# Another order of steps in attention, and the last unit's addition split over two engines, in an adaLN block with segment-memory attention and a SwiGLU network

## Chip, cores and metric

One core of a Trainium2 chip. The metric is the device time of one execution in microseconds (us); before the change its median is 1815.66 us over 3 runs (1815.52 to 1815.91).

## What is computed

All data are float32. 2048 tokens of width 576 pass a modulated layer norm, attention with 32 heads of 18 elements in four segments of 512 tokens, a projection with a gated residual, a second modulated layer norm and a SwiGLU network of width 4608. The reference, cut to what matters:

```python
mod = (_silu(c) @ w_mod).reshape(c.shape[0], 6, 1, -1)
sa, ca, ga, sb, cb, gb = ...
h = _layernorm(x) * (1 + ca) + sa
x = x + ga * _A_ref(h, wq, wk, wv, wo, beta)
h = _layernorm(x) * (1 + cb) + sb
x = x + gb * _B_ref(h, w_gate, w_up, w_down)      # (silu(h @ w_gate) * (h @ w_up)) @ w_down
...
for s in range(N):                                # _A_ref: four segments
    a_dot = softmax(qs @ ks^T * scale + mask) @ vs
    a_mem = (phi(qs) @ M) / (phi(qs) @ z + 1e-6)  # memory of the segments before
    o = g * a_mem + (1.0 - g) * a_dot
    M = M + phi(ks)^T @ vs
    z = z + sum(phi(ks))
...
return o @ wo
```

The gated output is the line `o = g * a_mem + (1.0 - g) * a_dot`.

## The kernel before, in words

Matrix products keep float32 accuracy by splitting each operand into a high and a low part (names ending in h and l) and adding three products. The program has three stages: projections of segments 0 to 2, attention (with the projections of segment 3, the output projection of finished segments and the preparation of the network's inputs woven in), and, behind the output projection of the last segment, the network.

**Attention** runs over 32 units, each one segment and four heads. Its order of work is written out by hand in the table ORDER: one string for each unit, with a token for each step. `<` and `>` ahead of a token move it to the unit before or behind. The tokens that matter here:

- `r` is a step of the maxima: one PSUM bank of scores (L689), whose row maxima VectorE takes with a custom reduction (L211). It works for the unit two further on. `s` is a step of the softmax: a bank of scores (L718) that ScalarE turns into exponentials (L725, L727); after some of them GpSimd cuts off the masked triangle (L730). When an `s` and an `r` stand next to each other, their matrix products are issued alternately.
- `m` transposes a unit's maxima (L235), `n` copies them (L239) and sends them by a DMA on SyncE's queue into two rows of that unit's `qs` tile (L194), which its `s` steps read.
- `V0123` multiplies the exponentials with the values (`av`, L744), `E` evacuates the product (`avs`, L757), `c` transposes it (`px`, L766) and `d` is comb_b: a reciprocal (L774), a product with it into `tmp` (L781) and the addition of `tmp` into the gated output `o` (L782). For segment 0 there is no addition. For the units behind, GpSimd adds; for the last unit, number 31, VectorE does.
- `M0` to `M3` and `X` are a half tile of the output projection (`pw`, L846) and its addition to the residual (`xr`, L851), `R S T Z z` make its operands (transposes L819 and L802, high parts L825, low parts L829), `l p x` are the second layer norm, and `y0` to `y131` are the steps that prepare the first half of the network's inputs: loads (L1143, L1146), transposes (L1155), scaling (L1150), GpSimd's sums (L1209), casts (L1134), low parts (L1117, L1119) and stores (L1123, L1125).

All banks of attention are one ring of eight in PSUM: a new one waits until the one eight places back has been read.

**Behind attention** the last segment's output projection stands in fixed order: TensorE transposes the gated output of the first 128 tokens (`pto`, four transposes L819), its last 64 columns for all tokens (`ptr`, L802) and the next 128 tokens, and then runs the projection's products (`pw`, L846). ScalarE casts the first transposes (`hh`, L825) before the products can begin. GpSimd's queue holds three sums for the network (L1221) and then four sums of weights (L1343). SyncE's queue loads weights (L1321) and the network's inputs `y` (L1308, L1309); the second of the weight tiles lies in memory that attention frees last. The first product of the network is an L1388 at 550.02 us.

Of the kernel before, what the change touches and what calls it, by code (L numbers as in the profile page):

```python
# [7 lines left out]
F32 = mybir.dt.float32  # L8
# [3 lines left out]
ALU = mybir.AluOpType  # L12
# [3 lines left out]
P = 128  # L16
S = 2048
D = 576
# [86 lines left out]
def block(ctx: ExitStack, tc: tile.TileContext, x, wqk, wv, wo, beta, wgu, wd, c, w_mod, wm01, out):  # L105
    nc = tc.nc
# [69 lines left out]
    NU = len(units)  # L176
    mcol, pmt, mrow, qe = {}, {}, {}, {}
    B1 = [[(3, h)] for h in (1, 0, 3, 2)] + [[(2, h), (0, h)] for h in (1, 0, 3, 2)] + [[(1, 1), (1, 3)], [(1, 0), (1, 2)]]
# [152 lines left out]
    with ExitStack() as p1:  # L331
# [3 lines left out]
        wk = pool(p1, "wk1", 2)  # L335
# [432 lines left out]
    def comb_b(u):  # L768
        if u < 0:
            return  # L770
        s, q = units[u]
# [1104 lines left out]
```

## Time and profile before

| | us |
|---|---|
| median of 3 runs | 1815.66 |
| the profiled execution's own time | 1815.06 |
| its span, first to last instruction | 1813.3 |
| attention's last `av` products end | 525.04 |
| first product of the last segment's projection | 532.52 |
| first product of the network | 550.02 |
| TensorE at half of its clock | 529.16 to 535.98 |
| mean granted clock over the span | 0.998 |

All times within the execution are counted from the span's start. PE is TensorE, PEld its loading of weights, DVE VectorE, ACT ScalarE, POOL GpSimd, SP SyncE. In a view of instructions in order of time, a line holds start, duration, engine, source line, operation, tiles (written<-read), sizes and count; a bracket at its end gives how long the engine stood idle ahead of it, and who ended that. A view of stretches gives the busy time of each engine in each stretch, with the number of its instructions in brackets, then the granted TensorE clock and the DMA engines' share.

### The profile page before, as it was taken

The numbers are of one execution on the slowest core, as the hardware profiler recorded it, in microseconds if no ns is written. First come the engines' busy times: TensorE is split into PE (matmuls) and PEld (weight loads), VectorE is DVE, ScalarE is ACT, GpSimd is POOL, SyncE is SP. The second block draws the span as 40 slices with busy tenths as digits, with TensorE's granted clock in tenths as the row PEclk, the third lists the DMA queues.
The fourth block names the chain that finished last, engine by engine and source line by source line (L and its number), as shares of the span: only waits on it lengthen the run. The fifth ranks groups of instructions, "written<-read, shape, count | busy, mean of one in ns | idle before, by whom it ended". The sixth has DMA issues, their size and how long they took to land.

```text
span 1813.3 us, 31111 instructions
## 1 busy us (share of the span) xinstructions
PE 1789.0 (99%) x11061; PEld 1515.2 (84%) x11061; DVE 1480.0 (82%) x3277; ACT 949.5 (52%) x2073; POOL 490.9 (27%) x707
## 2 busy tenths in 40 slices
PE   8999999999989999999999999999999999999999
PEld 5888867767778888888888888888888888888888
DVE  7567589999968888889888898668888888888886
ACT  6444578778866445444544444434544544544542
POOL 3000146555660544544454444100000000000000
PEclk9999999999999999999999999999999999999999
DMA  8678766577678455555544543594324324323331
GB/s 287 234 239 281 236 195 180 165 195 214 179 238 269 160 185 175 164 172 188 190 144 140 174 155 121 193 293 138 107 79 130 107 80 130 107 81 129 107 103 53
DMA packets 178563, 304.51 MB, mean 168 GB/s; under 512 B 25304, under 2 KB 108184, under 8 KB 176616
## 3 DMA queue, kind: packets, MB, share of 16 engines
q1 hardware_dynamic: 151032, 248.66, 43.9%
q10 hardware_dynamic: 27376, 53.86, 8.5%
q8 instruction: 88, 1.44, 0.3%
q14 instruction: 67, 0.55, 0.1%
HBM read 188.42 MB, written 113.33 MB: 166 GB/s over the span
## 4 chain that ended last, share of the span: by engine, by line
PE 68%; DVE 2%; DMA 1%; POOL 1%; issue 1%; ACT 1%; ACTq 0%; DVEq 0%
PE A L1388 24%; PE pd L1516 13%; PE C L1388 12%; PE pd L1497 10%; PE B L1388 6%; PE pw L846 1%; DMA y<-yD 1%; DVE wr L1338 0%; DVE wl L1353 0%; DVE dl L1378 0%; PE pt L1288 0%; ACT Pt L725 0%; PE av L744 0%; POOL Pt L730 0%; DVE acc L1526 0%
## 5 line engine op out<-in xcount | busy, mean ns | idle before, releaser
L1388 PE MATMUL A<-y,wh 128*128 128x512 f32 x1152 | 406.1, 393 | 1.2 <-ACT B L1434 0.9
L1388 PEld LDWEIGHTS A<-y,wh 128*128 128x128 f32 x1152 | 216.6, 188 | 46.2 <-ACT B L1434 2.4
L1353 DVE TENSOR_TENSOR wl<-O,wh 128x256 fp32r<-128x256 f32 x504 | 248.0, 497 | 2.1 <-ACT wh L1352 1.6
L211 DVE CUSTOM_DVE_ANT_0 junk<-s,tri 128x384 bf16<-128x384 f32 (+3 forms) x512 | 218.6, 486 | 25.2 <-PE s L689 12.7
L1388 PE MATMUL A<-y,wl 128*128 128x512 f32 x576 | 226.9, 394 | 0.0
L1502 DVE TENSOR_TENSOR acc<-acc,pd 128x576 f32<-128x576 f32 x216 | 162.4, 752 | 59.0 <-PE pd L1497 51.5
L1388 PE MATMUL C<-y,wh 128*128 128x512 f32 x576 | 203.0, 393 | 0.5 <-DVE cu L1411 0.5
L1352 ACT CAST wh<-O 128x256 fp32r<-128x256 f32 x504 | 197.6, 405 | 1.5 <-DMA yD<-st 1.2
L1526 DVE TENSOR_TENSOR acc<-acc,pd 128x576 f32<-128x576 f32 x156 | 116.9, 750 | 89.7 <-PE pd L1516 89.3
L1516 PE MATMUL pd<-dh,ah 128*128 128x288 f32 x640 | 189.0, 295 | 0.5 <-DVE x L1520 0.5
L1516 PE MATMUL pd<-dh,al 128*128 128x288 f32 x640 | 189.1, 296 | 0.0
L1516 PE MATMUL pd<-dl,ah 128*128 128x288 f32 x640 | 188.8, 295 | 0.0
L1343 POOL TENSOR_TENSOR O<-O 128x384 f32<-128x384 f32 x132 | 149.1, 1144 | 139.0 <-DMA O<-in_wgu_dram 64.3
L1457 ACT CAST ah<-sg 128x512 fp32r<-128x512 f32 x192 | 119.2, 621 | 77.9 <-DVE sg L1412 71.4
L725 ACT ACTIVATE Pt<-s 128x512 f32<-128x512 f32 x256 | 136.0, 599 | 21.4 <-PE s L718 15.2
L1458 DVE TENSOR_TENSOR al<-sg,ah 128x512 fp32r<-128x512 f32 x192 | 136.4, 710 | 10.4 <-ACT ah L1457 10.2
L1497 PE MATMUL pd<-dh,ah 128*128 128x288 f32 x448 | 133.0, 297 | 0.0
L1497 PE MATMUL pd<-dh,al 128*128 128x288 f32 x448 | 132.5, 296 | 0.0
L1497 PE MATMUL pd<-dl,ah 128*128 128x288 f32 x448 | 132.3, 295 | 0.0
L1516 PEld LDWEIGHTS pd<-dl,ah 128*128 128x128 f32 x640 | 120.5, 188 | 7.2
L1516 PEld LDWEIGHTS pd<-dh,ah 128*128 128x128 f32 x640 | 120.8, 189 | 6.8 <-DVE x L1520 0.8
L1388 PEld LDWEIGHTS C<-y,wh 128*128 128x128 f32 x576 | 108.3, 188 | 21.5 <-DVE cu L1411 1.2
(412 smaller groups left out, 4336.6 us busy)
## 6 DMA issues: line engine op xcount, KB each, us to landing
O<-in_wgu_dram SPq DMA_DIRECT2D x36, 768.0 KB
O<-oD SPq DMA_DIRECT2D x36, 512.0 KB
oD<-O ACTq DMA_DIRECT2D x34, 512.0 KB
ks<-kD SPq DMA_DIRECT2D x64, 216.0 KB
qs<-qD SPq DMA_DIRECT2D x64, 216.0 KB
O<-in_wgu_dram SPq DMA_DIRECT2D x36, 384.0 KB
rD<-wr ACTq DMA_DIRECT2D x36, 336.0 KB
wr<-rD SPq DMA_DIRECT2D x35, 336.0 KB
```

Source lines behind the costliest of these rows:

```text
L211: nc.vector.tensor_tensor_reduce(junk[:, :n], bank[:, o:o + n], tri[:, L - n:], 1.0, -3e38, op0=ALU.add, op1=ALU.max, accum_out=mcol[u][0] ...
L725: nc.scalar.activation(pt[:, h], bank, AF.Exp, scale=SCALE)
L1343: eng.tensor_tensor(o[:, d], o[:, a], o[:, b], op=op)
L1352: nc.scalar.copy(wh, o)
L1353: later.append(lambda: nc.vector.tensor_tensor(wl, o, f32(wh), op=ALU.subtract))
L1388: nc.tensor.matmul(bank, lhsT=a, rhs=b, start=(first and n == 0), stop=(n == 6), skip_group_check=not first)
L1457: nc.scalar.copy(ah, src)
L1458: later.append(lambda: nc.vector.tensor_tensor(al, src, f32(ah), op=ALU.subtract))
L1497: nc.tensor.matmul(pd[:, i, :288], lhsT=a[:, tk], rhs=w, start=(k == 0), stop=(k == 2))
L1502: nc.vector.tensor_tensor(o, o, pd[:, :, :288], op=ALU.add)
L1516: nc.tensor.matmul(pd[:, i, :288], lhsT=a[:, tk], rhs=w, start=(k == 0), stop=(k == 5))
L1526: nc.vector.tensor_tensor(o, o, pd[:, :, :288], op=ALU.add)
```

## The change

The first part rewrites ORDER from the second string on. It has the same tokens for the same units in all (the `y` steps have no unit), in another sequence; 260 pairs of neighbouring `s` and `r` become 259. TensorE's instructions stay 9,012 rows of the same matrix products. One string, the old and the new, and the second part in full:

```diff
-    "s s r s s y52 r r m U n V0123 l y59 E s r y83 s r s r M0 M1 y71 r s s r r s M2 y94 M3 X y106 y95 >r",
...
+    "s y52 s s r p y83 y49 y66 r s <E y84 V0123 y59 E r s s r s r M0 y106 M1 r s r s r s y77 M2 >U M3 y94 y95 y72 X y78 y119 >r",
...
         else:
-            tmp = wk.tile([P, 320], F32, tag="tmp", name="tmp")[:, :288].rearrange("p (i h z) -> p i h z", i=4, h=4)
+            last = u == NU - 1
+            tmp = (wk.tile([P, D], F32, tag="woraw", name="tmp", bufs=1) if last else
+                   wk.tile([P, 320], F32, tag="tmp", name="tmp"))[:, :288].rearrange("p (i h z) -> p i h z", i=4, h=4)
             nc.vector.tensor_tensor(tmp, v[:, :, :, :DH], rb, op=ALU.mult)
-            (nc.vector if u == NU - 1 else nc.gpsimd).tensor_tensor(dst, dst, tmp, op=ALU.add)
+            k = 3 if last else 4 if u == NU - 3 else 0
+            if k:
+                nc.vector.tensor_tensor(dst[:, :k], dst[:, :k], tmp[:, :k], op=ALU.add)
+            if k < 4:
+                nc.gpsimd.tensor_tensor(dst[:, k:], dst[:, k:], tmp[:, k:], op=ALU.add)
```

Each unit's output has four token blocks of 72 columns. VectorE now adds the first three blocks of unit 31 and GpSimd the fourth; unit 29 (NU - 3) is added by VectorE alone, where GpSimd did it before; the other units stay with GpSimd. The last unit's `tmp` takes a buffer of its own (the tag `woraw`, one buffer that the layer norm's output uses earlier), instead of the two that the units take in turn. The new lines shift the numbers: L782 becomes L786 (VectorE) and L788 (GpSimd), L781 becomes L783, and every line behind is 6 higher (L846 becomes L852).

VectorE's instructions at the end of attention, before, up to the low part of the projection's first operand (`r` and `tmp` belong to units 29, 30 and 31, in this order; `yo` and `yq` are low parts for the network):

```order
L774 RECIPROCAL r_8393<-px 128x16
L781 TENSOR_TENSOR tmp<-px,r_8393 128x288
L1119 TENSOR_TENSOR yo<-yh_5574,yo 32x256
L774 RECIPROCAL r_8404<-px 128x16
L781 TENSOR_TENSOR tmp<-px,r_8404 128x288
L774 RECIPROCAL r_8416<-px 128x16
L781 TENSOR_TENSOR tmp<-px,r_8416 128x288
L782 TENSOR_TENSOR o_6413<-o_6413,tmp 128x4x72
L829 TENSOR_TENSOR hl<-pto,hh 128x512
```

VectorE at the same place in the changed kernel:

```order
L774 RECIPROCAL r_8371<-px 128x16
L783 TENSOR_TENSOR tmp<-px,r_8371 128x288
L786 TENSOR_TENSOR o_6401<-o_6401,tmp 128x4x72
L1123 TENSOR_TENSOR yo<-yh_5626,yo 128x256
L1125 TENSOR_TENSOR yo<-yh_5627,yo 32x256
L774 RECIPROCAL r_8404<-px 128x16
L783 TENSOR_TENSOR tmp<-px,r_8404 128x288
L774 RECIPROCAL r_8416<-px 128x16
L783 TENSOR_TENSOR tmp<-px,r_8416 128x288
L786 TENSOR_TENSOR o_6401<-o_6401,tmp 128x3x72
L835 TENSOR_TENSOR hl<-pto,hh 128x512
```

Unit 29's addition and one more low part have come in ahead of unit 30; the last addition has three blocks instead of four.

GpSimd at the end of attention, before (the x2 are units 29 and 30; L1221 are the three sums for the network):

```order
L730 AFFINE_SELECT Pt<-Pt 128x4x128 x4
L1209 TENSOR_TENSOR yh_5571<-yh_5571,yh_5573 128x256
L1209 TENSOR_TENSOR yh_5571<-yh_5571 96x256
L1209 TENSOR_TENSOR yh_5571<-yh_5571,yh_5574 96x256
L782 TENSOR_TENSOR o_6413<-o_6413,tmp 128x4x72 x2
L1221 TENSOR_TENSOR ys<-yh_5571,yh_5572 128x512
L1221 TENSOR_TENSOR o_6413<-yh_5571,yh_5573 128x512
L1221 TENSOR_TENSOR ys<-yh_5571,yh_5574 96x512
```

GpSimd at the same place in the changed kernel:

```order
L730 AFFINE_SELECT Pt<-Pt 128x4x128 x4
L1215 TENSOR_TENSOR yh_5624<-yh_5624,yh_5626 128x256
L1215 TENSOR_TENSOR yh_5624<-yh_5624,yh_5627 96x256 x2
L788 TENSOR_TENSOR o_6401<-o_6401,tmp 128x4x72
L788 TENSOR_TENSOR o_6401<-o_6401,tmp 128x72
L1227 TENSOR_TENSOR ys<-yh_5624,yh_5625 128x512
L1227 TENSOR_TENSOR o_6401<-yh_5624,yh_5626 128x512
L1227 TENSOR_TENSOR ys<-yh_5624,yh_5627 96x512
```

Unit 29's addition is gone, and a quarter of unit 31's stands ahead of the three sums, which therefore wait for the last `tmp`.

TensorE where unit 31's maxima are transposed (`pmt`), before; the next `s` reads the tile of the unit ahead, `qs_996`, and three of unit 31's own (`qs_2347`) follow behind 16 `av` and 12 more `s`:

```order
L766 MATMUL px<-ident,avs 128x128 x4
L235 MATMUL pmt<-ident,mc 32x128
L718 MATMUL s_8163<-qs_996,ks_997 128x512
L718 MATMUL s_8166<-qs_996,ks_997 128x512
L718 MATMUL s_8173<-qs_996,ks_997 128x512
L718 MATMUL s_8176<-qs_996,ks_997 128x512
L744 MATMUL av<-Pt,vq_5821 32x512 x4
```

TensorE at the same place in the changed kernel:

```order
L766 MATMUL px<-ident,avs 128x128 x4
L1161 MATMUL pt<-ident,yq 96x128 x4
L235 MATMUL pmt<-ident,mc 32x128
L744 MATMUL av<-Pt,vq_5633 32x512 x4
L744 MATMUL av<-Pt,vq_5633 32x384 x4
L744 MATMUL av<-Pt,vq_5633 32x256 x4
L744 MATMUL av<-Pt,vq_5633 32x128 x4
L718 MATMUL s_8191<-qs_996,ks_997 128x512
```

The `av` products moved ahead of the four `s`; behind those, a half tile of the projection (14 `pw`) and four transposes now stand ahead of unit 31's first `s` as well, which before stood behind it.

56 rows, old and new, of the table ORDER are left out of this document.

## Prediction

> **What bounds the kernel now.** First the page's busy times: TensorE works 99% of the span.
>
> ```profile
> PE 1789.0 (99%) x11061; PEld 1515.2 (84%) x11061; DVE 1480.0 (82%) x3277; ACT 949.5 (52%) x2073; POOL 490.9 (27%) x707
> ```
>
> So a gain must come from TensorE's idle time or from its clock; the change leaves its products as they are. Next, the stretches: attention (to 525), the last segment's projection (525 to 550), the network's start.
>
> ```profile
> 215.00:525.00 310.00, 305.67 (x2867) 219.81 (x2865) 268.49 (x1127) 237.13 (x487) 176.10 (x379) 1.00 0.65 188
> 525.00:550.00 25.00, 21.11 (x144) 20.24 (x141) 18.47 (x32) 11.49 (x23) 10.50 (x11) 0.86 1.01 351
> 550.00:570.00 20.00, 20.00 (x89) 16.38 (x88) 17.23 (x36) 13.94 (x33) 0.00 (x0) 1.00 0.79 245
> ```
>
> Attention loses 4.3 of 310 us. The 25 us behind it lose 3.9 us and run at 0.86 of the clock. That joint is where the change's second part lies. TensorE there, in order of time:
>
> ```profile
> 520.47 4.57 PE L744 MATMUL av<-Pt,vq 128*32 128x512 f32 x64
> 525.85 0.66 PE L766 MATMUL px<-ident,avs 128*128 128x128 f32 x4 [0.22 <-ACT avs L757]
> 530.72 0.45 PE L819 MATMUL pto<-ident,o 128*128 128x128 f32 x1 [3.27 <-DVE o L782]
> 532.52 0.59 PE L846 MATMUL pw<-woh,hh 128*128 128x288 f32 x1
> ```
>
> And VectorE, GpSimd and ScalarE at that place:
>
> ```profile
> 525.66 0.26 DVE L774 RECIPROCAL r<-px 128x16 f32<-128x16 f32 x1 [3.24 <-PE px L766]
> 526.03 0.46 DVE L781 TENSOR_TENSOR tmp<-px,r 128x288 f32<-128x288 f32 x1
> 526.54 0.26 DVE L774 RECIPROCAL r<-px 128x16 f32<-128x16 f32 x1
> 527.10 0.46 DVE L781 TENSOR_TENSOR tmp<-px,r 128x288 f32<-128x288 f32 x1 [0.30 <-POOL o L782]
> 527.59 2.98 DVE L782 TENSOR_TENSOR o<-o,tmp 128x288 f32<-128x288 f32 x1
> ```
>
> ```profile
> 526.28 1.54 POOL L782 TENSOR_TENSOR o<-o,tmp 128x288 f32<-128x288 f32 x2
> 527.78 1.26 POOL L1221 TENSOR_TENSOR ys<-yh,yh 128x512 f32<-128x512 f32 x1
> 529.00 1.26 POOL L1221 TENSOR_TENSOR o<-yh,yh 128x512 f32<-128x512 f32 x1
> 530.22 1.47 POOL L1221 TENSOR_TENSOR ys<-yh,yh 96x512 f32<-96x512 f32 x1
> ```
>
> ```profile
> 531.20 0.58 ACT L825 CAST hh<-pto 128x512 fp32r<-128x512 f32 x1 [5.41 <-PE pto L819]
> ```
>
> The chain is: transposes of unit 31, reciprocal, `tmp`, addition, transposes `pto`, cast, products. VectorE's addition takes 2.98 us beside GpSimd's sums and ends 0.35 us after the third of them began. Its own work is a fraction of that: the low parts 128x256 from two SBUF tiles take 0.40 us, and when one of them meets a GpSimd sum it takes 0.83 us, which is the rest of that one sum plus its own time.
>
> ```profile
> L1117 DVE TENSOR_TENSOR mbd<-yh,mbd 128x256 fp32r<-128x256 f32 x4 | 1.6, 403 | 0.0
> ```
>
> ```profile
> 513.25 0.83 DVE L1117 TENSOR_TENSOR yo<-yh,yo 128x256 fp32r<-128x256 f32 x1 [2.22 <-ACT yo L1134]
> 513.05 1.62 POOL L1209 TENSOR_TENSOR yo<-yh,yo 128x256 f32<-128x256 f32 x2
> ```
>
> Last, the clock: half of it was granted for 6.82 us, shown here in halves, with stretches of the same length around them:
>
> ```profile
> 522.33:525.74 3.41, 3.30 (x52) 1.46 (x43) 0.17 (x2) 2.11 (x4) 3.33 (x6) 1.00 0.90 275
> 525.74:529.16 3.42, 1.20 (x7) 0.78 (x7) 2.93 (x5) 0.05 (x1) 3.42 (x5) 1.00 0.95 319
> 529.16:532.57 3.41, 1.85 (x10) 1.74 (x10) 2.10 (x2) 1.10 (x2) 3.41 (x3) 0.50 1.01 405
> 532.57:535.98 3.41, 3.41 (x16) 3.41 (x15) 1.38 (x2) 1.69 (x4) 3.01 (x4) 0.50 1.02 339
> 535.98:539.40 3.42, 3.42 (x29) 3.42 (x28) 2.37 (x5) 0.88 (x2) 0.00 (x0) 1.00 1.04 359
> ```
>
> A stretch with 1.20 us of work was followed by half the clock, one with 1.85 us did not end that, a full one did. At half clock 16 products run where 29 run at the full one.
>
> **The change part by part.** *The last addition.* (1) Unit 31's `tmp` no longer waits for GpSimd: it starts behind its reciprocal, at 526.83 instead of 527.10, 0.27 us earlier. (2) Three blocks of four on VectorE: between 0.34 us (216/256 of 0.403) and 2.98 us (the row as it is, if GpSimd keeps it out again). I take 0.36 us, near the lower end: GpSimd's sums can no longer start ahead of it, since its quarter, which waits for the same `tmp`, stands before them. That saves 2.62 us. `pto` then resumes at 530.72 - 0.27 - 2.62 = 527.83. (3) GpSimd's quarter: between 0.20 us (a quarter of the 0.80 us in the row below) and 0.80 us. Only the last `ptr` transpose needs it. I take 0.25 us behind VectorE's part, so 527.95 us; TensorE gets there at about 528.2 us, so it costs nothing, and 0.5 us at the upper end.
>
> ```profile
> L782 POOL TENSOR_TENSOR o<-o,tmp x23: 788/803/912, 321.8 to 527.0; 128x288 f32<-128x288 f32 x23
> ```
>
> The Trainium skill, page "SBUF — State Buffer", section "Who interferes with whom", says that a VectorE instruction with two SBUF inputs and a GpSimd instruction that reads SBUF exclude each other, and that the later one waits for the whole of the earlier. By that rule sharing runs no two parts at once, so 0.36 + 0.25 us would be no better than VectorE's undivided 0.46 us. The trace agrees that the two exclude each other, but the 2.98 us spans two whole sums, one more than the rule's words give.
>
> (4) From the resumed `pto` to the first product: 1.80 us now, at half clock. At full clock four transposes take 0.36 us of TensorE (the next product starts at 505.34), so the nine left take 0.81 us; the cast is later: 0.33 us for the transpose at full clock, 0.03, then 0.58 and 0.05 us, about 1.0 us. Saved 0.8 us.
>
> ```profile
> 504.98 0.60 PE L819 MATMUL pto<-ident,o 128*128 128x128 f32 x4
> 505.34 0.38 PE L846 MATMUL pw<-woh,hh 128*128 128x288 f32 x1
> ```
>
> (5) Products from 532.57 to 535.98 at full clock: 3.41 x (1 - 16/29) = 1.53 us saved, if the clock stays. In the stretch that now has 1.20 us of work, the nine transposes and some products would add 1.3 us: 2.5 of 3.41. Between 1.85, which did not raise the clock, and the 3.30 that kept it, the trace does not say; I take it as kept, because work that keeps the clock need not be as much as work that raises it.
>
> *Unit 29's addition* goes from GpSimd (0.80 us) to VectorE (0.46 us alone, up to about 1.3 us behind one GpSimd instruction). VectorE's 3.24 us of idle time ahead of 525.66 hides it; without that cover unit 30's reciprocal would be up to 1.3 us late, and all of (1) behind it. GpSimd then comes to unit 30's addition without a backlog.
>
> *What starts earlier.* GpSimd's three sums start about 0.2 us later (527.95 against 527.78) and VectorE reads them long after. The second weight load on SyncE's queue is issued right as the addition ends (530.57) and comes earlier with it:
>
> ```profile
> 530.65 0.33 SPq L1321 DMA_DIRECT2D O<-in_wgu_dram  x1
> 550.02 0.39 PE L1388 MATMUL A<-y,wh 128*128 128x512 f32 x1
> ```
>
> The DMA engines are full from 525 to 550 (share 1.01, 351 GB/s). What is loaded there is three `xr` and a fourth (288 KB each), two weight tiles (768) and four `y` (1216): 7.55 MB, about 22 us from 523.2, done at about 546. The last `y` is first read some 4.8 us into the network, 549.7 us if all moves up by 5.2 us. So 3 to 4 us of slack remain; TensorE's only wait of that kind now is 0.2 us, late in the program.
>
> *The new order.* TensorE's work is equal, so only its waits can change. Its twelve listed waits in attention before the joint add to 4.1 us; first, third and last:
>
> ```profile
> PE s L718 <- ACT Pt L727: 0.7, 1, 0.7
> ...
> PE s L718 <- DMA qs<-mr: 0.4, 2, 0.2
> ...
> PE s L689 <- DVE mx L211: 0.2, 1, 0.2
> ```
>
> If all vanish, 4.1 us are gained; as much again might come at other places, since VectorE is at 268.49 of 310 us and a bank read late stops the ring. The wait for unit 31's maxima goes (0.2 us: 16 `av` and more stand in its place), and I find no term that outweighs it; I take 0, with both ends for the range.
>
> **Sum:** 0.27 + 2.62 + 0.8 + 1.53 = 5.2 us. The profiled execution of 1815.06 us (a span of 1813.3 with 1.8 around it) would take 1809.8 us; the shown median is 0.6 us above it, so 1815.66 - 5.2 = **1810.5 us**.
>
> **The rivals.** *A, the clock falls all the same.* From the last `av` (525.04) to the first product (528.85) lie 3.8 us with transposes alone, longer than one stretch. For it: the stretch with seven transposes and no product was followed by half the clock. Against it: the work in it would double. Price: one stretch at half clock, 1.53 us, so 1812.0 us. The Trainium skill, page "TensorE: Matmul & The Clock Gate", section "Part 4: PE-mode transpose", says that transposes do not count as busy as products do, which would make A the case; no stretch here tells the kind of work apart from its amount.
>
> *B, the sharing does not do what it says.* GpSimd's unit 30 addition starts behind `tmp` at about 526.56 and ends at 527.36, just as VectorE's addition starts (527.32). If GpSimd's quarter and sums then follow without a gap, VectorE is kept out as before: 2.62, 0.8 and 1.53 us stay lost, and 1815.4 us results. Against it: at 513.25 VectorE got in between two GpSimd sums.
>
> *C, the order brings new waits* of 2 to 4 us. For it: TensorE's waits are few now, so that a new sequence can hardly remove many, and between two units' `av` more of VectorE's work may gather. Price 3 us: 1813.5 us.
>
> *D, slower.* One mechanism: the ring of eight banks, where VectorE's reductions and low parts hold banks that `s` and `r` need. VectorE has 310 - 268.49 = 41.5 us free in 31 units, 1.3 us each. If the sequence lets it fall behind in every unit, each costs TensorE a wait; from 0.3 us a unit (9 us in all, against 5.2 us gained) it is over 0.2% slower: about 1819.5 us. Against it: the single waits now are 0.2 to 0.7 us, twelve in 31 units.
>
> **How the numbers follow.** Forecast 0.50 (1808.4 to 1812.0), A 0.20, B 0.08, C 0.15, D 0.07. The range goes from 1808.0 (2.5 us of attention's waits gone as well) to 1815.4 (B), and leaves out D and the tails. A difference of 0.2%, 3.6 us, is about what a measurement of this kernel can tell from no change, so faster ends at 1812.0 us: the forecast and half of A, 0.60; half of A, B and C, 0.33; D, 0.07.
>
> **What would show it.** In the changed profile: the addition of 128x216 on VectorE near 0.36 us and no wait over 0.5 us of `pto` for it (1, 2); the first product about 3.8 us behind the last `av` instead of 7.5 (4); no half clock near 529 us (5; if it is there, A); GpSimd's sums behind the quarter (if VectorE's addition is over 2 us, B); attention's `av` end at 525.0 within 1 us (if it is later, C or D); no DMA wait of the network's first products. The prediction is wrong if attention itself moves by more than 2 us either way.

## Result, and the profile after

| | before | after |
|---|---|---|
| median, us | 1815.47 (1813.66 to 1818.79, 20 runs) | 1810.8 (1807.86 to 1815.57, 20 runs) |
| profiled execution, us | 1815.06 | 1811.66 |
| its span, us | 1813.3 | 1809.9 |

The ratio is 0.9975, with a 95% interval from 0.9968 to 0.9982: the changed kernel is faster by about 4.7 us, over the 0.2% (3.6 us) that the prediction calls the least a measurement can tell; the interval's weak end, 0.18%, lies just under it. (The ratios, here and below, are not exactly the quotients of the two medians.) Its median came out 0.3 us from the forecast. The parts did not, and most of what follows is about them.

The page's busy times of the changed kernel:

```profile
PE 1784.7 (99%) x11061; PEld 1512.8 (84%) x11061; DVE 1479.9 (82%) x3278; ACT 947.8 (52%) x2073; POOL 492.3 (27%) x707
```

The three stretches that were shown of before:

```profile
215.00:525.00 310.00, 306.67 (x2892) 221.85 (x2890) 274.83 (x1141) 238.61 (x492) 179.06 (x381) 1.00 0.66 191
525.00:550.00 25.00, 22.52 (x154) 21.27 (x155) 20.56 (x39) 13.72 (x29) 9.30 (x9) 1.00 1.01 362
550.00:570.00 20.00, 18.86 (x82) 15.15 (x81) 16.92 (x34) 12.14 (x29) 0.00 (x0) 1.00 0.89 303
```

The clock of the 25 us behind attention is 1.00 instead of 0.86. But TensorE is still idle for 2.5 us there, and for 1.1 us in the 20 us behind, which had no idle time before. Fixed stretches hide what moved, since the work in them shifts, so the table below cuts each trace at the same instructions: the first product of segment 3's projections, the end of the last `av`, the first product of the last segment's projection, and the network's 1st, 141st, 1501st and 2001st product, counting the products of L1388 (L1394 in the changed kernel) alone. But for the last `av`, whose end counts, the marks are starts.

| stretch, us | before | after | difference |
|---|---|---|---|
| stage 1 (its code is unchanged) | 194.31 | 196.66 | +2.35 |
| attention, to the last `av` | 330.73 | 326.30 | -4.43 |
| joint, to the projection's first product | 7.48 | 3.85 | -3.63 |
| projection, to the network's first product | 17.49 | 18.12 | +0.63 |
| network, products 1 to 140 | 38.75 | 39.67 | +0.92 |
| to product 1500 | 496.40 | 496.04 | -0.36 |
| to product 2000 | 182.19 | 183.35 | +1.16 |
| the rest | 545.98 | 545.95 | -0.03 |

They add up to the 3.4 us between the spans. Stage 1 takes 192.8 to 198.8 us in the fourteen profiles of this study although no kernel changes it, and 192.8 to 196.7 us in the three of the changed kernel (after, e4, e11). Part of that is the clock: in the changed kernel, e7 and e10 half of it was granted for 3.4 or 6.8 us from 151 us on, and these three have the longest stage 1 (196.7 to 198.8 us; the other eleven 192.8 to 194.8). This is why each step is judged by its own stretch and not by the span.

**The joint.** TensorE of the changed kernel in order of time:

```profile
522.89 0.66 PE L766 MATMUL px<-ident,avs 128*128 128x128 f32 x4
523.83 0.66 PE L766 MATMUL px<-ident,avs 128*128 128x128 f32 x4 [0.28 <-ACT avs L757]
525.42 0.72 PE L825 MATMUL pto<-ident,o 128*128 128x128 f32 x4 [0.93 <-DVE tmp L783]
525.97 0.60 PE L808 MATMUL ptr<-ident,o 128*64 128x128 f32 x4
...
526.81 0.40 PE L852 MATMUL pw<-woh,hh 128*128 128x288 f32 x1
```

VectorE and GpSimd there:

```profile
524.81 0.46 DVE L783 TENSOR_TENSOR tmp<-px,r 128x288 f32<-128x288 f32 x1
525.30 0.38 DVE L786 TENSOR_TENSOR o<-o,tmp 128x216 f32<-128x216 f32 x1
```

```profile
524.43 1.45 POOL L788 TENSOR_TENSOR o<-o,tmp 128x288 f32<-128x288 f32 x2
525.84 1.27 POOL L1227 TENSOR_TENSOR ys<-yh,yh 128x512 f32<-128x512 f32 x1
...
531.86 4.88 POOL L1349 TENSOR_TENSOR O<-O 128x384 f32<-128x384 f32 x4 [2.22 <-DMA O<-in_wgu_dram]
```

VectorE's three blocks take 0.38 us; GpSimd's sums start at 525.84, behind both additions. The last row is new: the sums of weights (L1349) wait 2.22 us for the first weight tile. GpSimd does not come to them earlier than before: counted from the last `av`, it ends the third sum at 6.65 us in the kernel before and at 6.68 us here. Before, the weights were there in time; here they are not.

**The clock at the joint.** In each of the fourteen traces the changes of the clock lie whole multiples of 3.413 us apart (in the changed kernel 11.38, 151.32, 154.74 and 1810.20 us). Cut by that grid, there are six stretches at full clock that hold transposes and no product: one in the changed kernel and in e8, which the full clock followed, and one in e2, e3, e5 (below, in this order) and the kernel before (525.74:529.16 in the prediction, 1.20 us of work), which half of it followed. The experiments are described further down.

```profile
523.38:526.79 3.41, 2.20 (x18) 1.69 (x16) 1.81 (x5) 1.01 (x3) 3.27 (x5) 1.00 0.89 274
```

```profile
522.19:525.60 3.41, 2.11 (x18) 1.66 (x17) 1.81 (x5) 1.01 (x3) 3.27 (x5) 1.00 0.84 258
```

```profile
521.70:525.11 3.41, 1.61 (x11) 0.93 (x9) 2.30 (x6) 0.67 (x1) 3.41 (x5) 1.00 0.84 258
```

```profile
520.96:524.37 3.41, 1.52 (x11) 1.10 (x12) 2.56 (x4) 0.11 (x1) 3.41 (x4) 1.00 0.88 270
```

```profile
526.95:530.37 3.42, 0.41 (x4) 0.44 (x5) 2.87 (x1) 0.07 (x1) 3.42 (x4) 1.00 0.95 329
```

So here transposes alone kept the clock, with 2.11 us of work in a stretch or more, and lost it with 1.61 us or less.

**The give-back.** ScalarE's cast of these sums, and TensorE in the projection behind it:

```profile
536.77 0.62 ACT L1343 CAST wr<-O 96x512 fp32r<-96x512 f32 x1 [3.69 <-POOL O L1349]
```

```profile
541.15 0.37 PE L852 MATMUL pw<-woh,hh 128*128 128x288 f32 x1 [2.06 <-DVE xr L857]
```

In the program's order, the projection's next cast (`hh`, L831) stands behind that cast on ScalarE, and runs at 537.60. VectorE waits 1.97 us for it:

```profile
538.21 0.69 DVE L835 TENSOR_TENSOR hl<-pto,hh 128x512 fp32r<-128x512 f32 x1 [1.97 <-ACT hh L831]
```

Behind this low part follow VectorE's addition to the residual (`xr`, 540.55), which empties TensorE's bank, and TensorE, after 2.06 us of waiting. The weight tile is late because of SyncE's queue:

```profile
522.35 0.36 SPq L1129 DMA_DIRECT2D yD<-yo  x1
523.22 0.31 SPq L1131 DMA_DIRECT2D yD<-yo  x1
523.58 1.39 SPq L819 DMA_DIRECT2D xr<-in_x_dram  x3
525.09 0.36 SPq L1327 DMA_DIRECT2D O<-in_wgu_dram  x1
```

The load goes behind two stores of network inputs (`yo`), 2.13 us after the last `av` (522.96). In the kernel before it went 0.56 us after it: the new order does these last steps later, relative to attention's end. In the network's first 140 products TensorE then waits 1.14 us for VectorE (`cu`, L1417), where it waited 0.48 us before.

### The profile page after: what moved, and what is told of

The parts are those of the page before. It is cut to its first block, busy times and chain, and to the rows that moved or that the text cites. A ratio compares the mean times of both kernels' runs of the same rounds, so it can differ in the third digit from the quotient of the medians.

```text
span 1809.9 us, 31119 instructions
## 1 busy us (share of the span) xinstructions
PE 1784.7 (99%) x11061; PEld 1512.8 (84%) x11061; DVE 1479.9 (82%) x3278; ACT 947.8 (52%) x2073; POOL 492.3 (27%) x707
## 3 DMA queue, kind: packets, MB, share of 16 engines
q8 instruction: 88, 1.44, 0.4%
## 4 chain that ended last, share of the span: by engine, by line
PE 80%; DVE 2%; DMA 2%; POOL 1%; issue 1%; ACT 1%; ACTq 0%; SPq 0%; POOLq 0%; DVEq 0%
PE A L1394 25%; PE pd L1522 14%; PE C L1394 12%; PE pd L1503 10%; PE B L1394 6%; PE av L744 3%; PE pw L852 3%; PE s L689 2%; PE s L718 2%; PE pn L988 1%; DMA y<-yD 1%; DMA O<-in_wgu_dram 1%; PE pw L929 1%; DVE junk L211 1%; PE px L766 1%
## 5 line engine op out<-in xcount | busy, mean ns | idle before, releaser
L1394 PE MATMUL A<-y,wh 128*128 128x512 f32 x1152 | 406.2, 393 | 2.4 <-DMA y<-yD 1.3
L1394 PEld LDWEIGHTS A<-y,wh 128*128 128x128 f32 x1152 | 216.6, 188 | 47.5 <-ACT B L1440 2.1
L1394 PE MATMUL A<-y,wl 128*128 128x512 f32 x576 | 226.9, 394 | 0.0
L1394 PE MATMUL C<-y,wh 128*128 128x512 f32 x576 | 202.9, 393 | 1.1 <-DVE cu L1417 1.1
L1349 POOL TENSOR_TENSOR O<-O 128x384 f32<-128x384 f32 x132 | 148.7, 1140 | 138.6 <-DMA O<-in_wgu_dram 48.5
L1394 PEld LDWEIGHTS C<-y,wh 128*128 128x128 f32 x576 | 108.3, 188 | 21.8 <-DVE cu L1417 1.6
```

The costliest lines, as they stand in the source:

```text
L1349: eng.tensor_tensor(o[:, d], o[:, a], o[:, b], op=op)
L1394: nc.tensor.matmul(bank, lhsT=a, rhs=b, start=(first and n == 0), stop=(n == 6), skip_group_check=not first)
```

## Experiments

Each run stands beside runs of the kernel before on the same chip. The medians of before were 1814.59 us beside e1 to e4, 1815.73 beside e5 to e8, 1815.44 beside e9 and e10, and 1816.27 beside e11 and e12.

### The two parts apart: e1, e2, and the change again: e4

e1 is the changed kernel with the old ORDER, e2 the kernel before with the new ORDER; e4 is the changed kernel once more.

Against the changed kernel, e1 (one string of ORDER) and e2 read:

```diff
-    "s y52 s s r p y83 y49 y66 r s <E y84 V0123 y59 E r s s r s r M0 y106 M1 r s r s r s y77 M2 >U M3 y94 y95 y72 X y78 y119 >r",
...
+    "s s r s s y52 r r m U n V0123 l y59 E s r y83 s r s r M0 M1 y71 r s s r r s M2 y94 M3 X y106 y95 >r",
```

```diff
-            k = 3 if last else 4 if u == NU - 3 else 0
...
+            (nc.vector if u == NU - 1 else nc.gpsimd).tensor_tensor(dst, dst, tmp, op=ALU.add)
```

> The old order of steps with the new addition (own buffer for the last unit, three blocks on VectorE and one on GpSimd, unit 29 on VectorE). If the gain comes from the joint behind attention, as predicted: about 5 us faster than before (1810.5), attention from the first projection of segment 3 to the last av as long as before (330.7 us), and 3.8 us instead of 7.5 from the last av to the first product. If the gain comes from the new order, as the pair of profiles suggests (330.7 us against 326.3): the joint is short, but at most 2 us are left at the end (1813.5), since the weights' sums on GpSimd wait for their load and give the rest back.

> The new order with the old addition (VectorE alone for unit 31, in the shared buffer, unit 29 on GpSimd). If the gain comes from the joint: no faster than 1 us below before (1814.5 to 1815.5). If it comes from the order: attention takes about 326.3 us and the median is 3 us or more below before (1812.5), while the joint keeps its addition of about 3 us and a half clock.

> The changed kernel once more, to see what its stages vary by. If attention's gain is the order's: 326 us again within 1 us from the first projection of segment 3 to the last av. If that was a chance of one execution: nearer to 330.7. The stages ahead of segment 3's projections, which the change leaves alone, show how much of the spread of about 2 us lies there. The first product is again about 3.8 us behind the last av if the addition is not kept out.

| | median, us | ratio to before | attention | joint | projection | products 1 to 140 |
|---|---|---|---|---|---|---|
| e1, additions alone | 1813.05 (11 runs) | 0.9984 (0.9974 to 0.9993) | 330.80 | 3.79 | 16.90 | 39.34 |
| e2, order alone | 1812.05 (11 runs) | 0.9985 (0.9976 to 0.9994) | 326.73 | 7.71 | 17.15 | 39.01 |
| e4, both | 1811.6 (10 runs) | 0.9977 (0.9967 to 0.9987) | 327.68 | 3.86 | 19.90 | 39.00 |

e1's median, 1813.05, is what was expected if the gain came from the order. e2's is 2.5 us below its kernel before, where 3 or more were expected of a gain by the order. e4's attention is 1.4 us longer than in the first profile of the same kernel, where 1 us was expected at most; its profile is of the slowest of its ten runs. By stretches the parts separate cleanly: the order shortens attention and leaves the joint alone (7.71 us, with VectorE's addition at 2.98 us again), the additions do the reverse. By medians each brings 1.5 to 2.5 us and both bring 3.0, with intervals too wide to say whether anything is lost in the sum. The stretches say it: from the last `av` to product 140 (joint, projection and products together) e1 takes 60.03 us, the changed kernel 61.64 and e4 62.76, against 63.72 before. With the new order, 1.6 to 2.7 us of what the additions gain is gone again by product 140 (in e4 with half of the clock for 3.4 us at 540.5 us).

### What keeps VectorE's addition out: e3, e5, e6

e3 is the changed kernel with all four blocks of unit 31 on VectorE, so that no quarter stands in GpSimd's queue:

```diff
-            k = 3 if last else 4 if u == NU - 3 else 0
+            k = 4 if last or u == NU - 3 else 0
```

> The changed kernel with all four blocks of unit 31 on VectorE, still in its own buffer. If sharing matters: the joint is longer than in the changed kernel, and GpSimd's sums start ahead of the addition and keep it out again (2 to 3 us, 1813). If only the order of GpSimd's queue and the buffer matter, the sums start earlier or later by chance: GpSimd's unit 30 addition ends about when VectorE's begins, so the addition takes either 0.5 us or over 1.7 us. If two SBUF readers exclude each other and VectorE gets in between two GpSimd instructions, 0.5 to 1.3 us, and the median is within 1 us of the changed kernel.

e5 takes the old ORDER, and of the second part the buffer alone:

```diff
-            k = 3 if last else 4 if u == NU - 3 else 0
+            k = 4 if last else 0
```

> The kernel before, with one thing of the second part only: unit 31's tmp in a buffer of its own. The addition of all four blocks stays on VectorE, unit 29's stays on GpSimd. Theory 1 (what costs is that GpSimd's sums follow one another without a gap and VectorE gets in only behind them): tmp starts 0.27 us earlier, the addition is kept out as before and still takes over 2 us, from the last av to the first product it is 7.0 to 7.5 us, half of the clock is granted near 529 us as before, and the median is within 1 us of the kernel before. Theory 2 (the early start alone lets VectorE in ahead of the sums): the addition takes about 0.5 us, the stretch about 4 us, no half clock there, and the median is 1.5 us lower, as with the whole second part.

e6 is the kernel before, with a copy of one column of the finished output ahead of GpSimd's three sums. Its result is not read; it only makes the sums wait for the last addition:

```diff
+        nc.gpsimd.tensor_copy(omg[:, 1:2], ot[3][:, 3, 575:576])
         for kb in range(3):
             y_sum(kb)
```

> The kernel before with one tiny GpSimd copy of a column of the finished gated output ahead of the three sums for the network, so that the sums begin only behind unit 31's addition; nothing else of the change. Theory 1 (the place of GpSimd's sums makes the wait, not the amount of VectorE's work): the whole addition of four blocks takes 0.5 us instead of 2.98, from the last av to the first product it is 4 to 5 us instead of 7.5, the clock stays full or falls for one window only, the span's gain in that stretch is 2.5 to 4 us, and the median is 1.5 to 3 us below the kernel before. Theory 2 (the smaller share of VectorE and the move of unit 29 to VectorE are what counts): 7.5 us as before and no gain. If the sums of weights behind it come later than their load, the projection stage grows by up to 1 us.

VectorE and GpSimd of e5 at the joint:

```profile
526.58 3.24 DVE L786 TENSOR_TENSOR o<-o,tmp 128x288 f32<-128x288 f32 x1
```

```profile
527.02 1.26 POOL L1227 TENSOR_TENSOR ys<-yh,yh 128x512 f32<-128x512 f32 x1
528.24 1.26 POOL L1227 TENSOR_TENSOR o<-yh,yh 128x512 f32<-128x512 f32 x1
529.46 1.49 POOL L1227 TENSOR_TENSOR ys<-yh,yh 96x512 f32<-96x512 f32 x1
```

And of e6:

```profile
526.51 0.55 DVE L782 TENSOR_TENSOR o<-o,tmp 128x288 f32<-128x288 f32 x1
```

```profile
527.12 0.19 POOL L1619 COPY omg<-o 128x1 f32<-128x1 f32 x1 [0.38 <-DVE o L782]
527.27 1.27 POOL L1221 TENSOR_TENSOR ys<-yh,yh 128x512 f32<-128x512 f32 x1
```

| | median, us | ratio to before | addition | joint | projection |
|---|---|---|---|---|---|
| e5, buffer alone | 1814.76 (10 runs) | 0.9996 (0.9987 to 1.0005) | 3.24 | 7.10 | 17.00 |
| e6, sums later | 1810.64 (9 runs) | 0.9972 (0.9962 to 0.9981) | 0.55 | 4.22 | 16.30 |
| e3, all on VectorE | 1810.15 (6 runs) | 0.9971 (0.9960 to 0.9982) | 1.44 | 5.33 | 17.33 |

In e5 the addition starts earlier and loses it all again: it spans the end of unit 30's addition and two whole sums and ends 0.36 us into the third. That end is 5.52 us behind the last `av`, 5.53 in the kernel before. In e6 the same undivided addition takes 0.55 us, and one column's copy brings about as much as the whole second part: joint -3.3 us and projection -1.2 us, where e1 has -3.7 and -0.6. Its median is 5.1 us below that of its kernel before, more than the 1.5 to 3 expected, and as far as the whole change comes with its new order (4.7 us). So the price was the place of GpSimd's sums, not the amount of VectorE's work and not the buffer. What the sharing does is to put an instruction that needs the last `tmp` ahead of the sums. In e3, without it, the first sum starts ahead of the addition and keeps it out once:

```profile
522.34 1.44 DVE L786 TENSOR_TENSOR o<-o,tmp 128x288 f32<-128x288 f32 x1
```

```profile
522.20 1.26 POOL L1227 TENSOR_TENSOR ys<-yh,yh 128x512 f32<-128x512 f32 x1
```

That costs 1.5 us at the joint; the 1.44 us lie between the ranges that were expected. e3's median is nevertheless not above that of e4, on the same chip; its intervals overlap with those of the others. A joint that ends earlier only meets the late weights. Why VectorE gets in behind one sum in e3 and behind two in e5 the traces do not say.

### Where the gain is given back: e7, e9, e10, e11, e12

e7 issues the first weight load ahead of the three loads of the residual.

```diff
-        xr3 = {i: load_xr(3, i) for i in range(3)}
...
         load_o(0, 0, 0)
+        xr3 = {i: load_xr(3, i) for i in range(3)}
```

> The changed kernel with the first weight tile's load issued ahead of the three loads of the residual instead of behind them, that is 1.4 us earlier on SyncE's queue. Theory 1 (part of the gain is given back because GpSimd's sums of weights wait for that load, ScalarE's cast for them, and TensorE for the addition to the residual behind it): GpSimd's wait falls from 2.22 us to about 0.8, TensorE's wait of 2.06 us in the projection falls below 1 us, the stretch from the projection's first product to the network's first is 17 us or less instead of 18.1 and 19.9, and the median is about 1 us below the changed kernel's (1809.5 to 1811). Theory 2 (the loads share full DMA engines, so what comes earlier for the weights comes later for the residual): TensorE waits as long, for the residual's load or its addition, and the stretch stays at 18 us or more.

The median was 1812.11 us (11 runs), ratio 0.9984 (0.9975 to 0.9993), above what theory 1 expected. The profile is of the slowest of the eleven (1817.75 us). In it, GpSimd's wait is gone, TensorE's wait in the projection is 0.2 us, and the projection takes 16.28 us, as theory 1 has it. Then the network's first 140 products take 44.93 us instead of 39.67. SyncE's queue, VectorE and TensorE of e7 there:

```profile
541.48 11.63 SPq L859 DMA_DIRECT2D xD<-xr  x4
```

```profile
570.12 1.15 DVE L1349 TENSOR_TENSOR O<-O 128x384 f32<-128x384 f32 x2 [2.88 <-DMA O<-in_wgu_dram]
```

```profile
574.07 0.73 PE L1394 MATMUL C<-y,wh 128*128 128x512 f32 x1 [3.81 <-DVE cu L1417]
```

The four stores of the residual take 11.63 us to get out, 5.54 in the changed kernel: one of them waits 9.8 us for a store of weights (`oD<-O`). The weight load behind them comes at 554.60 us, 29.4 us behind the last `av` where it is 27.8 in the changed kernel (550.72 - 522.96). VectorE waits 2.88 us for it, and TensorE 3.81 us for VectorE. So moving one load ahead of three others mended one wait and made a larger one, on the same queue, in this run; whether the others lost as much is not shown.

e9 leaves the loads where they are and moves what stands ahead of them. One token of ORDER goes ahead of unit 31's last four exponentials: y111, ScalarE's cast of the last 128-row input. VectorE's, GpSimd's and SyncE's orders stay as they are. e11 is the changed kernel and e12 is e9's kernel once more, both on one chip.

```diff
-... y130 s y124 >X s s s y131 s y115 V0123 y111 y89 y128 <d E ...
+... y130 s y111 y124 >X s s s y131 s y115 V0123 y89 y128 <d E ...
```

> The changed kernel with one token of ORDER moved: y111, ScalarE's cast of the last 128-row input for the network, stands ahead of unit 31's last four exponentials instead of behind them (beside y124). VectorE's order, GpSimd's and SyncE's stay; on SyncE's queue the last two stores of network inputs can go earlier, and with them all the loads behind. In the changed kernel the first weight load goes 2.1 us behind the last av, with the old order 0.2 to 0.9 us behind it. Theory 1 (the new order's late stores hold up the loads, and that gives part of the gain back): VectorE's low part comes at about 520 instead of 521.5, the load about 0.5 us behind the last av, GpSimd's wait for it falls from 2.2 us to under 1, TensorE's wait of 2.1 us in the projection falls to under 1, the three stretches from the last av to the network's 140th product take 59 to 60 us instead of 61.6, and the median is 1.5 to 2.5 us below the changed kernel's, about 1809. Theory 2 (the DMA engines are full there, so an earlier start only spreads the same waits): the three stretches stay at 61 us or more and the median within 0.7 us of the changed kernel's.

> The changed kernel as it is, beside the next run on the same chip. Both theories: median 1810 to 1812 us; in the profile attention 326 to 328 us, last av to first product 3.8 to 3.9 us, the first weight load 2.1 us behind the last av, GpSimd's wait for it above 2 us.

> The same kernel as e9 (one token moved: the last 128-row cast ahead of unit 31's last four exponentials), now beside the changed kernel on one chip. Theory 1 (the late stores hold the loads up): 1.5 to 3 us below the changed kernel's median, the first weight load 0.5 to 1.4 us behind the last av, GpSimd's wait for it about 1 us, projection 16.5 to 17.5 us. Theory 2 (e9's lower median came from the chip and the draw of runs): within 0.7 us of the changed kernel.

e10 joins the new ORDER with e6's copy, with the additions as before.

> The new order, the old addition (all of unit 31's on VectorE, unit 29's on GpSimd, no buffer of its own), and the tiny GpSimd copy that keeps the three sums behind the last addition. Theory 1 (the joint's gain comes from the place of the sums, attention's from the order, and the two add up except for the loads): attention 326 to 327.7 us, last av to first product about 4.2 us, projection 18 us or more because the weights still arrive late, median 1810 to 1811.5, as the changed kernel. Theory 2 (the rest of the second part, the shared addition and unit 29's move, brings something of its own): 1 us or more above the changed kernel.

SyncE's queue and GpSimd in e12:

```profile
522.88 0.33 SPq L1327 DMA_DIRECT2D O<-in_wgu_dram  x1
```

```profile
529.26 5.32 POOL L1349 TENSOR_TENSOR O<-O 128x384 f32<-128x384 f32 x4
```

| us | median | ratio to before | load behind last `av` | attention | joint | projection | products 1 to 140 | last three together |
|---|---|---|---|---|---|---|---|---|
| e11, changed kernel | 1809.03 (5 runs) | 0.9964 (0.9951 to 0.9976) | 2.12 | 326.18 | 3.85 | 18.42 | 39.99 | 62.26 |
| e9 | 1808.04 (6 runs) | 0.9958 (0.9944 to 0.9972) | 1.28 | 329.16 | 3.85 | 17.32 | 40.99 | 62.17 |
| e12, as e9 | 1808.23 (5 runs) | 0.9957 (0.9943 to 0.9970) | 0.34 | 328.52 | 3.85 | 16.39 | 38.77 | 59.01 |
| e10 | 1812.01 (9 runs) | 0.9975 (0.9963 to 0.9987) | 2.13 | 326.52 | 4.44 | 18.01 | 39.02 | 61.47 |

e11 repeats the changed kernel's stretches as expected, with a median 1 us below the expected range. In e12 the load goes 0.34 us behind the last `av`, GpSimd's wait is gone, TensorE's is down from 2.4 to 0.3 us, and the three stretches take 59.01 us, 3.25 less than in e11: theory 1, for the load, the waits and the projection. e9's profile, of the slowest of its six runs, shows it half done, and its 62.17 us for the three stretches is what theory 2 expected there, although the median, 1808.04, is theory 1's: the load goes 1.28 us behind, GpSimd waits 1.1 us and TensorE 1.3 us, and later TensorE waits 1.8 us for VectorE's `cu` and gets half of the clock for 3.4 us at 570 us. The token has a price of its own: GpSimd's cut of the last exponentials comes later, and the last `av` wait 0.5 us for it. The other 1.6 us (e12) and 2.3 us (e9) by which attention is longer than in the changed kernel's first profile arise before the moved token, at steps that all of them share (e9: 1.5 us for `vt`; e12: 0.9 us for `avs`); the changed kernel itself varies so, 327.68 us in e4. On one chip e12's median is 0.8 us below e11's, between the two theories (1.5 to 3 and within 0.7), with intervals that overlap. That its tail is shorter is shown; that the kernel as a whole is faster than the changed one is not.

e10 gives what the two mechanisms predict: the order's attention, e6's joint, the late weights (2.0 us of TensorE's wait in the projection), and the changed kernel's ratio, 0.9975; its median, 1812.01, lies 0.5 us above theory 1's range. Sharing the addition brings nothing beyond e6's copy that these runs can tell. Nor does the new order, by these medians: e10 has it on top of e6's kernel, attention is 4.7 us shorter, the three stretches 2.2 us longer (61.47 against 59.27), and the ratios, 0.9975 and 0.9972, cannot be told apart.

One number sums them up: from the first weight load to the network's first product it is 19.8 to 20.3 us in the changed kernel, e1, e6, e8, e9, e10, e11 and e12, whether the load goes 0.2 or 2.2 us behind the last `av` (24.4 us before, 23.2 in e5 and 22.7 in e2, where the joint is long; 21.6 in e4 and 20.5 in e3, with half of the clock in between; 19.5 in e7, where the load stands elsewhere). TensorE's own work from the last `av` to that product takes 20.2 us (e12, without such a wait). So in these kernels a load that goes later than about 0.4 us behind the last `av` adds its lateness; e12 against e11 shows it by a single step, the other profiles only agree.

### Where in attention the order gains: e8

e8 is the changed kernel with the first 12 strings of the old ORDER; up to there both orders have done the same steps.

> The changed kernel with the old order for the first 12 strings, the new order for the other 20; up to there both orders have done the same steps. In the profiles the new order is 0.9 us ahead after 12 strings and 4.4 us at the end. Theory 1 (the order's gain is a few waits and better pairing at single places of the later strings): attention takes 327 to 328 us, against 330.8 with the old order and 326.3 to 327.7 with the new one. Theory 2 (it comes evenly with the units): 12 of 32 strings fall away, about 1.6 us, so 328 to 329 us. Theory 3 (the order pays only as a whole): 330 us or more. The median lies within 1 us of the changed kernel's for the first, above it for the others.

Attention takes 328.12 us, the median is 1810.68 us (10 runs), ratio 0.9973 (0.9964 to 0.9982). This lies on the edge between theories 1 and 2 and does not tell them apart; theory 3 falls. At equal counts of `s` products, the changed kernel is 0.9 us ahead of the kernel before behind string 12 and wins 3.5 us more behind it; e8 is 0.7 us late behind string 12 and wins 3.3 us behind it. So the gain of the later strings does not need the earlier ones. How much the earlier strings bring is open: behind string 12 the changed kernel's own repeat, e4, is level with the kernel before. e8's last three stretches take 63.32 us, 1.7 us more than the changed kernel's, with the load 2.24 us behind the last `av`.

What is won can be read from TensorE's waits in attention and from its busy time. The changed kernel's five listed waits there add to 2.2 us, where the kernel before had twelve lines with 4.3 us:

```profile
PE av L744 <- ACT Pt L725: 0.6, 1, 0.6
PE pt L1161 <- DMA yh<-xh: 0.5, 1, 0.5
PE pw L852 <- DVE mx L211: 0.4, 1, 0.4
PE pp L876 <- DVE mbd L546: 0.4, 1, 0.4
PE pw L929 <- DVE mx L211: 0.3, 1, 0.3
```

TensorE's busy time in attention to the last `av`, in the kernel before and in the changed one (stretch, its length, busy time with the number of records, clock, DMA share, GB/s):

```profile
194.30:525.00 330.70, 326.36 (x2969) 1.00 0.66 193
```

```profile
196.66:522.96 326.30, 323.77 (x2969) 1.00 0.67 194
```

Both stretches hold 2969 records. Of the 4.4 us, 1.8 us are idle time (4.3 against 2.5 us), and 2.6 us are busy time: the same products, laid closer. It is the `s` and `r` products that lie closer. In the view of single instructions an `s` and an `r` product of a pair start within 0.01 us of each other and run side by side; the time that at least one of them (L718, L689) covers is 111.6 to 112.2 us in the four profiles of the old order and 108.6 to 109.4 in the seven of the new one, while their durations add to 336.7 to 337.0 and 336.2 to 336.7 us, and all other products cover 227.4 to 228.1 and 227.4 to 227.9 us. Why they overlap better no run tested; that the bank ring stalls less would fit.

## Why the prediction was right or wrong

- **The wait for the buffer (0.27 us).** Right that the wait goes: GpSimd does not end it any more, and `tmp` starts 1.85 us behind the last `av` instead of 2.06. By itself that is worth nothing: in e5 the addition ends as late as before, and the 0.38 us by which e5's joint is shorter arise behind it, where the clock fell 6.07 us behind the last `av` instead of 4.12.
- **The addition (0.36 instead of 2.98 us).** Right: 0.38 us, because the sums stand behind the quarter. e6 shows the reason by itself.
- **The quarter (hidden).** Right in that nothing waits for it: `ptr` follows the first four `pto` at once. The 0.93 us of wait ahead of the first `pto` is ended by `tmp`; the fourth, which needs the addition, follows with no listed wait, where it waited 3.27 us.
- **From `pto` to the first product.** Right: 3.85 us from the last `av`, 3.8 forecast.
- **The clock (1.53 us).** Right in kind, against rival A: no half clock at the joint in any of the ten profiles with a joint of 3.8 to 4.5 us; with 7.48 and 7.71 us it lasted 6.8 us, with 7.10 and 5.33 us it lasted 3.4. In the ten no stretch of the grid that touches the joint has less than 2.00 us of work, so it was not luck of where the grid fell. The size is nearer to 1.2 us: e6 and e7, at full clock and with 0.2 us of wait, take 16.3 us for the projection, the kernel before 17.49. The Trainium skill, page "TensorE: Matmul & The Clock Gate", section "Part 4: PE-mode transpose", says that transposes do not count as busy as products do; by the stretches of the changed kernel and of e8, which hold transposes alone (2.20 and 2.11 us) and kept the clock, they counted here.
- **Unit 29's addition (up to 1.3 us, hidden).** It took 2.11 us behind GpSimd's work, more than the bound, and VectorE then stood idle for 1.72 us, so it is hidden all the same.
- **What starts earlier (no cost).** Wrong, and this is the step that failed: "3 to 4 us of slack remain" was worked out for the last `y` load. The first thing that needs a load is GpSimd's sum of weights, and by ScalarE's queue the projection hangs on it. It had next to nothing to spare: in e1, whose load goes 0.92 us behind the last `av` instead of 0.56, GpSimd already waits 0.74 us, and in the changed kernel 2.22 us, TensorE 2.06. What the new order does to SyncE's queue (the last two stores late, the load 2.1 instead of 0.6 us behind the last `av`) was not looked at, though VectorE's rows in the section on the change show the low parts of `yo` come in behind unit 29's addition.
- **The new order (0 us, bounds 4.1).** Wrong, and over its bound: 4.4 us, 4.3 on average over seven profiles with the new order (326.62 us) against four with the old (330.89). "I find no term that outweighs it" looked for single waits (the rows of its list add to 4.3 us, not 4.1); more than half came from products laid closer, which no listed wait shows (e8's section). By the prediction's last sentence (attention within 2 us) it is wrong in this step: equal work does not mean equal busy time.
- **The sum.** 5.2 us were forecast from the joint and its clock alone. The joint gave 3.6 of the 3.7 us forecast for it, the clock about 1.2 of 1.53. Attention's 4.4 us came on top, and 2 to 3 us went back behind the joint: in the projection 1.8 us above the 16.3 us of e6 and e7, and 1 us in the network's first products. The rest is stage 1 and the later network, which vary from profile to profile by up to 6 and 4 us with no change in their code. So the median came out right by luck: two errors of opposite sign, 4.3 us too little for attention and 2 to 3 us too much behind the joint.
- **The rivals.** A falls (above). B's mechanism is real, e5 shows it with an addition of 3.24 us, but the quarter prevents it. C and D fall: attention became shorter in every profile with the new order or most of it (326.2 to 329.2 us).

## What to carry to other kernels

When two engines keep each other out, as VectorE's addition and GpSimd's sums do here, look at what stands next in the other engine's queue: one small instruction that waits for the critical result, ahead of a run of long ones, was worth as much as dividing the work. When a joint becomes shorter, list every load that is issued behind it, find its first reader on each engine, and recompute the slack for that reader; loads issued behind stores on one queue went as late as the stores did. A new order should be judged by busy time over equal work too, not by listed waits alone.

## What the hardware showed beyond that

- VectorE's addition of 128x288 from two SBUF tiles took 0.46 us by itself (unit 29 in e1), 0.55 us behind the end of one GpSimd instruction, 1.44 us behind one sum, and 2.98 and 3.24 us behind two. The Trainium skill, page "SBUF — State Buffer", section "Who interferes with whom", lets the later of the two wait for the whole of the earlier. That fits 1.44 us; 2.98 and 3.24 us are longer, since the next sum got in ahead of VectorE.
- Half of the clock came in pieces of 3.4 or 6.8 us, on a grid of 3.413 us that is fixed in each trace. What counted was TensorE's work within one stretch of that grid, and not the length of a wait: a wait of 2.33 us that left 1.25 us of work in its stretch brought it (e4, at 540.5 us), one of 2.38 us that lay across two stretches, with 1.94 and 2.50 us of work, did not (e11). Over all fourteen traces, from 15 to 1800 us, every stretch at full clock with less than 1.54 us of work was followed by half of the clock; from 1.54 to 1.76 us both happened; of those with more, one was (2.30 us, e10 at 147.5 us). Why that one was is open.
